# The V half of a gated MLP worked in PSUM from batch 1 on, three remainders moved to GpSimd, and another order of the steps

## The chip, the core and the metric

The kernel runs on one core of a Trainium2 chip. Its time is the device time of one execution in microseconds (us); the time before is the median of 3 runs, 585.59 us (585.12 to 588.33). One more execution was taken by the profiler, and all rows below come from that.

## What is computed

Pooled attention followed by a gated MLP, for 8 batches of 576 positions. Keys and values are averaged over groups of 8 positions; each of 8 heads (64 wide) attends to the 72 pooled keys. The output is the MLP's input `x` (576 x 512).

```python
k_p = k.reshape(B, H, Sp, pool, D).mean(axis=3)
v_p = v.reshape(B, H, Sp, pool, D).mean(axis=3)
attn = softmax(q @ k_p.T / sqrt(D))            # 1e-9 added to the sum
x = (attn @ v_p) as (batch, 576, 512)
h = gelu(x @ w_in)                             # 576 x 1024
u, v = h[..., :512], h[..., 512:]
v_n = (v - mean(v)) / sqrt(var(v) + 1e-6) * g_ln
v_s = w_sg @ v_n + b_sg                        # mixes the 576 positions
out = x + (u * v_s) @ w_out
```

## The kernel before

Every float32 product is made of three products in a rounded form that TensorE takes: a value is written as `hi` (a cast by ScalarE) and a remainder `lo` (value minus `hi`, by GpSimd or VectorE), and hi x hi, hi x lo and lo x hi are added up in PSUM. So nearly every result passes ScalarE and GpSimd once before TensorE can use it.

The work of a batch is cut into named steps, written as generators; each `yield` ends a part. A: load keys, B: load values, C: load queries, E: load the left-over pooled rows, K: pool keys, P: pool values, Q: transpose queries, S: scores and softmax (one for each pair of heads), L and T: transpose the probabilities, V: attention times values, H: the V half of `x @ w_in` with gelu and normalisation, U: the other half with gelu, W: the mixing product with the gate, G and O: the output product (batches 1 to 6 use a form with seven quarter products instead of eight), Z: transpose and store.

Four lists of tokens (PROLOGUE, FIRST, PERIOD, LAST) give the order in which the parts are issued: `H4+0` advances step H4 of the current batch by one part, `S2+1` step S2 of the next. PERIOD is used five times, for batches 2 to 6; the others serve batch 0 (with the conversion of the weights), batch 1 and batch 7. Within each engine the instructions run in the order of the lists, so an instruction that waits holds up all that stands behind it on its engine. All loads and stores are issued on SP's queue, also in this order.

PSUM is handled as four slots `ps` of two banks each. A step takes the slot that has been free the longest (`take`) and returns it (`give`) after the instruction that reads it last.

Step H (from line 712) makes one tile of 128 rows of `x @ w_in` for the V half, in five row tiles H0 to H4. Tile 4 has 64 rows, and its product comes in two halves of the partitions that have to be added. Its parts are: 12 matmuls; for tile 4 a copy of one half to SBUF (L740) and the addition (L742); gelu from PSUM to SBUF (L747, tile 4 L745); statistics `bn_stats` and `bn_aggr` on VectorE (L752, L753) and two small steps on GpSimd for `rstd` (L755, L756); the normalise, one tensor_scalar on VectorE (L758); the cast `hi` on ScalarE (L761); the remainder `lo` (L763), on GpSimd for tiles 0 to 3 and on VectorE for tile 4. From the gelu on the tile lies in SBUF, in a free part of `xmem` (the other batch's input and result) or, for tile 4, in `left`; the slot is given back at the gelu, or for tile 4 at the addition.

Step W (from line 792) mixes the positions: 28 matmuls that read the tiles of H in order, those of tile 4 (`vtail`) last; then the gate on VectorE (L822, L824). Step S: five matmuls for the scores, the maximum (L547), ten exponentials on ScalarE (L566) with their sums, then on VectorE the addition of 1e-9 (L575), the reciprocal (L581) into PSUM beside the scores, the multiply (L584), after which the slot is given back, and two copies `el` on GpSimd (L592). Step P, part 2, makes the pooled values' `vbh` and `vl` (ScalarE, L494 and L508) and their remainders (VectorE, L503 and L510). Step Z transposes on VectorE (L988) into two quarters of `umem` in turn and stores these, so the third and fourth transposes wait for the stores of the first two.

Of the kernel before, what the change touches and what calls it, by code (L numbers as in the profile page):

```python
# [28 lines left out]
T2+0 K2+1 K2+1 B0+1 V3+0 Q1+1 v2 S0+1 V1+0 v2 V3+0 V2+0 C2+1 S0+1 V3+0 P1+1 S0+1 V0+0 S1+1 V2+0 V0+0 C3+1 V3+0 S1+1  # L29
Q2+1 S1+1 lu1 u0 S0+1 S0+1 V2+0 H1+0 u1 S1+1 u0 S0+1 u0 H1+0 u1 S1+1 u0 S1+1 V0+0 H0+0 S0+1 H2+0 S2+1 u1 S1+1 Q3+1  # L30
P0+1 T0+1 V2+0 V1+0 H0+0 u0 u3 u2 u3 u3 H2+0 T0+1 S2+1 S3+1 C0+2 S0+1 H4+0 S3+1 u3 T0+1 S2+1 H3+0 P2+1 S3+1 H4+0 S2+1
H4+0 u3 u2 S3+1 P2+1 u2 H3+0 lo0 S2+1 U1+0 S2+1 S3+1 u2 U3+0 H0+0 H1+0 S2+1 U1+0 S3+1 H4+0 P2+1 U3+0 lo1 u2 H2+0 o0
H3+0 A1+2 o1 H4+0 C2+2 S3+1 H0+0 U0+0 H2+0 H3+0 H0+0 lb0 A0+2 H1+0 o1 H2+0 H4+0 H1+0 P2+1 S3+1 U0+0 U2+0 S2+1 S1+1
H0+0 K0+2 H4+0 o0 E0+2 H4+0 C1+2 H1+0 H2+0 H3+0 L0+1 L0+1 L0+1 U2+0 H3+0 B0+2 L0+1 o1 T1+1 o0 W0+0 K1+2 V0+1 o1 o1
T1+1 V0+1 T1+1 K2+2 o0 o0 o3 o3 W0+0 o3 W3+0 o2 W2+0 V1+1 W3+0 o2 T2+1 T3+1 K2+2 K2+2 o2 V1+1 V0+1 T2+1 W3+0 W0+0 o2
B1+2 Q0+2 W2+0 W2+0 W1+0 T2+1 V2+1 K2+2 K2+2 Q1+2 T3+1 W1+0 W1+0 S1+2 W0+0 W2+0 T3+1 V1+1 S0+2 V2+1 W1+0 P0+2 C3+2
S0+2 o3 V3+1 W3+0 O1+0 C0+3 V3+1 V2+1 V3+1 O1+0 Q2+2 O0+0 O1+0 S1+2 S0+2 o2 Z1+0 O0+0 O0+0 S0+2 S2+2 Z0+0 A0+3 S2+2
# [3 lines left out]
H3+0 O3-1 O3-1 r0 r0 r0 S2+1 r0 H2+0 r0 S1+1 V2+0 P2+1 P2+1 r1 r1 Z1-1 S2+1 K0+2 V0+0 H4+0 r1 P2+1 r1 H1+0 Q0+2 Z2-1
T0+1 H3+0 O3-1 H2+0 H0+0 Z3-1 r3 H4+0 H2+0 Z2-1 H0+0 r3 H3+0 r3 H0+0 S3+1 H4+0 S3+1 H4+0 H1+0 H4+0 S3+1 H3+0 H4+0 H2+0
B0+2 T0+1 r3 H0+0 U1+0 H1+0 U3+0 r2 U2+0 H4+0 H3+0 S3+1 P2+0 U0+0 H0+0 H1+0 H4+0 S0+1 H3+0 H1+0 E0+2 H0+0 H1+0 S3+1
U2+0 U3+0 Z3-1 W1+0 U1+0 r2 K1+2 r2 U0+0 T0+1 r2 r2 K2+2 L0+1 W0+0 W2+0 W1-1 W1+0 W0+0 T0+1 L0+1 L0+1 K2+2 W3+0 W2+0
G0+0 G1+0 L0+1 G0+0 W3+0 L0+1 L0+1 T1+1 V0+1 G1+0 G1+0 S2+0 T2+1 G2+0 G2+0 T1+1 O1+0 T1+1 G2+0 V0+1 G3+0 G4+0 S1+0
V1+1 T2+1 T2+1 K2+2 G2+0 V1+1 G3+0 K2+2 B1+2 O0+0 G2+0 C1+2 T3+1 G4+0 K2+2 C2+2 G3+0 V2+1 O0+0 V2+1 T3+1 G4+0 O0+0
O2+0 O0+0 G4+0 O2+0 V1+1 O0+0 S0+2 T3+1 O0+0 S2+0 O1+0 V3+1 V0+1 O1+0 G4+0 S0+2 O1+0 O0+0 Z0+0 V3+1 Z0+0 Z1+0 O0+0
Z1+0 Z2+0 V3+1 S1-1 Z3+0 Q1+2 V2+1 Z2+0 Z3+0
# [5 lines left out]
S3+1 W1+0 W0+0 P2+1 S2+1 U2+0 S3+1 T0+1 A0+2 W1+0 U3+0 P2+1 T0+1 G1+0 U3+0 W3+0 L0+1 G0+0 G0+0 L0+1 K0+2 K1+2 W2+0
T1+1 P2+1 L0+1 G1+0 L0+1 T2+1 G1+0 W3+0 L0+1 W2+0 G2+0 V0+1 L0+1 G2+0 E0+2 G2+0 T1+1 O1+0 T1+1 V0+1 K2+2 V1+1 T2+1
K2+2 T2+1 O0+0 G3+0 O0+0 G2+0 V1+1 G3+0 W1-5 V2+1 C0+2 T3+1 T3+1 G2+0 T3+1 G3+0 O0+0 G4+0 K2+2 V3+1 O0+0 V2+1 G4+0
O0+0 O0+0 G4+0 O2+0 G4+0 V0+1 O1+0 V3+1 K2+2 O2+0 Q0+2 O1+0 B1+2 K2+2 O1+0 G4+0 Z1+0 O0+0 Z0+0 C2+2 S0+2 O0+0 S0+2
Z0+0 V2+1 V1+1 Z1+0 Z2+0 Z3+0 W0-4 B0+2 Z3+0 Z2+0 V3+1
# [1001 lines left out]
```

## Time and profile before

| | |
|---|---|
| median of 3 runs | 585.59 us |
| the profiled execution | 585.92 us |
| its span (first to last instruction) | 584.1 us |
| mean granted TensorE clock | 0.976 |
| busy: TensorE, VectorE, ScalarE, GpSimd | 95%, 75%, 64%, 58% |

The profile's times are microseconds from the start of the span unless a row says ns. PE is TensorE, DVE VectorE, ACT ScalarE, POOL GpSimd, SP the engine that issues the DMAs. A granted clock of 1.00 is the upper of TensorE's two levels, 2.4 GHz; 0.50 would be the lower, 1.2 GHz. "L758" is line 758 of the kernel; all matmuls have line 133, a helper. `ps` is any of the four slots, `vk` the buffer of the normalised tiles.

### The profile page before, as it was taken

To read this page: it belongs to the slowest core of one execution; us is meant where nothing else is said; L and a number is where in the kernel's file an instruction comes from. 1 tells how busy PE (TensorE), PEld (TensorE's weight loads), DVE (VectorE), ACT (ScalarE), POOL (GpSimd) and SP (SyncE) were. 2 spreads that over 40 slices of the span, in tenths; PEclk is the share of its full clock that TensorE was granted. 3 is DMA by queue.
4 is the path that set the end of the run, shared out by engine and by line. 5 is a ranking of instruction groups with operands and counts; after the bars stand their busy time and mean duration, and the time that the engine had idled before them with its cause. 6 is when DMAs were issued, how large, how long until landed. Compare 5 with 4: busy or idle time off the path is not lost.

```text
span 584.1 us, 10533 instructions
## 1 busy us (share of the span) xinstructions
PE 554.8 (95%) x3675; PEld 518.3 (89%) x3675; DVE 439.5 (75%) x592; ACT 373.1 (64%) x979; POOL 337.9 (58%) x383
## 2 busy tenths in 40 slices
...
GB/s 251 345 183 282 93 75 48 97 115 78 38 82 66 79 96 42 89 128 72 96 26 108 140 41 102 45 99 142 60 82 68 120 81 12 10 1 82 2 1 81
DMA packets 199428, 53.43 MB, mean 91 GB/s; under 512 B 181712, under 2 KB 186896, under 8 KB 199376
## 3 DMA queue, kind: packets, MB, share of 16 engines
...
## 4 chain that ended last, share of the span: by engine, by line
PE 65%; DVE 21%; issue 6%; DMA 2%; ACT 2%; POOL 2%; SPq 1%; DVEq 0%; ACTq 0%; POOLq 0%
PE ps L133 62%; DVE vp L406 4%; DVE left L758 3%; PE ps L169 2%; DVE nmax L547 2%; DVE bst L752 2%; DVE e L584 2%; SPq L221 1%; DMA left<-in_moe_w_sg 1%; DVE xmem L910 1%; DVE xmem L758 1%; DVE vk L763 1%; DMA left<-in_k 1%; DVE qbuf L529 1%; ACT umem L778 1%
## 5 line engine op out<-in xcount | busy, mean ns | idle before, releaser
L133 PE MATMUL ps<-wsh,vk 128*128 128x288 f32 x512 | 105.0, 316 | 4.9 <-DVE e L584 3.4
L133 PEld LDWEIGHTS ps<-wsh,vk 128*128 128x128 f32 x512 | 85.1, 205 | 7.3 <-issue 4.5
L133 PE MATMUL ps<-xhlk,wih 128*128 128x288 f32 x512 | 89.9, 298 | 0.2 <-DVE e L584 0.2
L133 PE MATMUL ps<-wih,xhlk 128*128 128x512 f32 x256 | 84.4, 400 | 0.4 <-DVE al L676 0.2
L566 ACT ACTIVATE e<-ps,nmax 128x72 f32<-128x72 f32 x240 | 73.0, 354 | 12.4 <-DVE nmax L547 12.3
L133 PEld LDWEIGHTS ps<-xhlk,wih 128*128 128x128 f32 x512 | 75.4, 188 | 1.2 <-issue 0.4
L755 POOL TENSOR_TENSOR rstd<-mv,eps 128x1 f32<-128x1 f32 (+1 forms) x40 | 10.2, 256 | 90.8 <-DVE mv L753 73.8
L133 PE MATMUL ps<-wsl,vk 128*128 128x288 f32 x256 | 61.1, 312 | 0.0
L133 PEld LDWEIGHTS ps<-wih,xhlk 128*128 128x128 f32 x256 | 48.1, 188 | 12.5 <-ACT xmem L747 1.0
L566 ACT ACTIVATION_READ_ACCUMULATOR e<-ps,nmax 128x1 f32 x240 | 57.5, 240 | 0.0
L133 PE MATMUL ps<-xhlk,wil 128*128 128x288 f32 x256 | 55.0, 296 | 0.0
L133 PE MATMUL ps<-wil,xhlk 128*128 128x512 f32 x128 | 50.6, 395 | 0.0
L592 POOL COPY el<-e 128x40 f32<-128x40 f32 x64 | 16.6, 322 | 51.7 <-DVE e L584 48.0
L910 DVE TENSOR_TENSOR xmem<-ps,xmem 128x576 f32<-128x576 f32 x42 | 31.4, 748 | 20.0 <-PE ps L133 19.7
L133 PEld LDWEIGHTS ps<-wsl,vk 128*128 128x128 f32 x256 | 46.1, 206 | 0.0
L133 PE MATMUL ps<-gk,woh 128*128 128x288 f32 x224 | 45.9, 296 | 0.0
L708 POOL TENSOR_TENSOR xhlk<-xmem,xhlk 128x576 fp32r<-128x576 f32 x32 | 45.1, 1430 | 1.2 <-ACT xhlk L706 1.2
L133 PE MATMUL ps<-kbd,qbuf 128*128 128x144 f32 x320 | 43.7, 287 | 1.1 <-ACT qbuf L523 0.9
L133 PEld LDWEIGHTS ps<-kbd,qbuf 128*128 128x128 f32 x320 | 41.6, 190 | 2.4 <-ACT qbuf L523 1.0
L854 POOL TENSOR_TENSOR umem<-umem 128x576 f32<-128x576 f32 x24 | 34.9, 1454 | 13.5 <-DVE umem L824 10.2
L763 POOL TENSOR_TENSOR vk<-xmem,vk 128x512 fp32r<-128x512 f32 x32 | 41.6, 1325 | 0.0
L133 PEld LDWEIGHTS ps<-xhlk,wil 128*128 128x128 f32 x256 | 41.0, 188 | 0.0
...
## 6 DMA issues: line engine op xcount, KB each, us to landing
...
```

The lines of the kernel that those rows point to most:

```text
L133: nc.tensor.matmul(o, lhsT, rhs, start=start, stop=stop, **flags)
L169: nc.tensor.transpose(ps[:rows, i * P:(i + 1) * P], src(i), ident if i < NT - 1 else swap)
L406: nc.vector.tensor_reduce(out=o, in_=t.rearrange("p a (r d) -> p a d r", r=POOL), axis=AX.X, op=ALU.add)
L547: nc.vector.tensor_reduce(out=nmax, in_=every.rearrange("p s (h k) -> p s h k", h=2), axis=AX.X, op=ALU.max, negate=True)
L566: nc.scalar.activation(e[:, i, h], slots[i][:, h], AF.Exp, bias=nmax[:, i, h:h + 1], **acc)
L584: (nc.gpsimd if (b, g) in MUL_POOL else nc.vector).tensor_tensor(e, e, rec.unsqueeze(3).broadcast_to([P, NT, 2, SP]), op=ALU.mult)
L592: nc.gpsimd.tensor_copy(st["el", b].rearrange("p t (n j a) -> p t n j a", n=2, a=4)[:, :, g // 2, :, 2 * (g % 2) + h], ef[:, :, LEFT[h]:LE ...
L708: nc.gpsimd.tensor_tensor(xhl[:, 1, g], x32[:, g], xhl[:, 0, g].bitcast(F32), op=ALU.subtract)
L758: nc.vector.tensor_scalar(vg, vg, mv[:, 0:1], rstd, op0=ALU.subtract, op1=ALU.mult)
L763: (nc.gpsimd if i < NT - 1 else nc.vector).tensor_tensor(lo, vg, hi.bitcast(F32), op=ALU.subtract)
L854: nc.gpsimd.tensor_tensor(x, p, q, op=ALU.subtract)
L910: nc.vector.tensor_tensor(x, ps[:, :, 0:HALF], x, op=ALU.add)
```

## The change

From batch 1 on (`old` is batch 0 alone) gelu writes its result back into the slot, statistics and normalise read it there, and the normalise writes to SBUF and gives the slot back. Tile 4's remainder goes to GpSimd from batch 1 on. From batch 2 on (`own`; LEFT_TE holds batches 0 and 1) the remainders `vbl` and `vl` of step P go to GpSimd; as GpSimd's subtraction takes no scale, ScalarE first scales `vp` in place. In the softmax of batches 2 to 7 the addition of 1e-9 writes into PSUM, and the reciprocal works there in place. All four lists hold the same tokens as before in another order; PROLOGUE is the same up to its 141st token.

```diff
@@ step_P
+        own = b not in LEFT_TE
+        if own:
+            nc.scalar.mul(vp, vp, 1.0 / POOL)
         for h in range(2):
             r = slice(D * h, D * h + D)
+            if own:
+                nc.scalar.copy(vbh[r, :, D * h:D * h + D], vp[r])
+                continue
             nc.scalar.mul((vb[b] if b in WHOLE else vbh)[r, :, D * h:D * h + D], vp[r], 1.0 / POOL)
...
+            if own:
+                nc.gpsimd.tensor_tensor(vbl[r, :, D * h:D * h + D], vp[r], vbh[r, :, D * h:D * h + D].bitcast(F32), op=ALU.subtract)
+                continue
...
-        nc.vector.tensor_tensor(vl[64:96], v32, vl[64:96].bitcast(F32), op=ALU.subtract)
+        (nc.vector if b in LEFT_TE else nc.gpsimd).tensor_tensor(vl[64:96], v32, vl[64:96].bitcast(F32), op=ALU.subtract)
@@ step_S
-            nc.vector.tensor_scalar(ssum, ssum, 1e-9, None, op0=ALU.add)
...
-        nc.vector.reciprocal(rec, ssum)
+        if mode:
+            nc.vector.reciprocal(rec, ssum)
+        else:
+            nc.vector.tensor_scalar(rec, ssum, 1e-9, None, op0=ALU.add)
+            nc.vector.reciprocal(rec, rec)
@@ step_H
+        old = b == 0
+        h = vg if old else o[:n]
         if i == NT - 1:
             nc.scalar.copy(vg, o[n:2 * n])
             yield
-            nc.vector.tensor_tensor(vg, o[:n], vg, op=ALU.add)
-            give(bank)
-            yield
-            nc.scalar.activation(vg, vg, AF.Gelu_apprx_tanh)
-        else:
-            nc.scalar.activation(vg, o, AF.Gelu_apprx_tanh)
+            nc.vector.tensor_tensor(h, o[:n], vg, op=ALU.add)
+            if old:
+                give(bank)
+            yield
+        nc.scalar.activation(h, o if old and i < NT - 1 else h, AF.Gelu_apprx_tanh)
+        if old and i < NT - 1:
             give(bank)
...
-        nc.vector.bn_stats(bst, vg)
+        nc.vector.bn_stats(bst, h)
...
-        nc.vector.tensor_scalar(vg, vg, mv[:, 0:1], rstd, op0=ALU.subtract, op1=ALU.mult)
+        nc.vector.tensor_scalar(vg, h, mv[:, 0:1], rstd, op0=ALU.subtract, op1=ALU.mult)
+        if not old:
+            give(bank)
...
-        (nc.gpsimd if i < NT - 1 else nc.vector).tensor_tensor(lo, vg, hi.bitcast(F32), op=ALU.subtract)
+        (nc.gpsimd if i < NT - 1 or b > 0 else nc.vector).tensor_tensor(lo, vg, hi.bitcast(F32), op=ALU.subtract)
```

In the middle batches the matmul parts follow each other so, before and after (one pass of PERIOD: H, U, W and O are of the current batch, T and V, and S1 to S3, of the next, the S0 at the end of the one after):

```
before: H2 H1 H0 S1 H3 H4 U1 U0 S2 S3 U2 W0 W1 U3 W3 W2 T1 T2 V0 O1 V1 O0 V2 T3 O0 V3 O0 O2 O1 O0 S0
after:  H0 H3 H1 H2 S1 U0 H4 U1 S3 S2 U3 U2 W1 W0 W3 W2 T1 T2 V0 O0 V1 O1 V2 T3 O0 V3 O0 O2 O1 S0 O0
```

VectorE's parts in the first half of the pass, from the new list: S0 multiply, H0 statistics, H3 statistics, H0 normalise, H1 statistics, H3 normalise, H1 normalise, S1 maximum, H2 statistics, Q3 and Q2 transposes, H2 normalise, P1 pooling, S1 multiply, H4 addition, S3 maximum, H4 statistics, T0 transpose, H4 normalise, S2 maximum, S3 multiply, P0 pooling, S2 multiply. ScalarE's: S1 exponentials, H4 copy, U0 gelu, H4 gelu, U1 gelu, H2 cast, S3 exponentials, H4 cast, S2 exponentials. GpSimd's before W: H1 and H3 `lo`, H4 `rstd`, H0 and H2 `lo`, S1 and S3 `el`, H4 `lo`, S2 `el`, then step P's three remainders.

## Rows read from the trace of the kernel before

**Rows 1.** The page, busy time, share of the span and instructions of each engine.
```profile
PE 554.8 (95%) x3675; PEld 518.3 (89%) x3675; DVE 439.5 (75%) x592; ACT 373.1 (64%) x979; POOL 337.9 (58%) x383
```
**Rows 2.** Waits of TensorE and VectorE: us in total, times, the longest.
```profile
PE ps L133 <- DVE vk L763: 14.2, 6, 2.5
PE ps L133 <- DVE e L584: 3.6, 6, 0.7
DVE umem L988 <- DMA out<-umem: 24.8, 12, 4.4
```
**Rows 3.** Timelines, batch 6: start, us, engine, instruction [idle before it <- until whom].
```profile
478.43 5.20 DVE L758 TENSOR_SCALAR left<-left,mv,rstd 64x512 f32<-64x512 f32 x1
488.97 0.69 DVE L763 TENSOR_TENSOR vk<-left,vk 64x512 fp32r<-64x512 f32 x1
...
478.37 4.98 POOL L763 TENSOR_TENSOR vk<-xmem,vk 128x512 fp32r<-128x512 f32 x4
...
489.71 0.53 PE L133 MATMUL ps<-wth,vk 128*128 128x288 f32 x2 [2.49 <-DVE vk L763]
```
**Rows 4.** Windows, two W steps each (columns in the rows' order: length, busy, PEclk).
```profile
207.41:220.08 12.67, 9.48 (x58) 9.05 (x57) 12.40 (x17) 12.50 (x50) 2.84 (x6) 0.87 0.33 96
276.30:288.75 12.45, 9.27 (x59) 8.82 (x57) 12.18 (x17) 12.29 (x49) 2.60 (x6) 0.86 0.32 97
344.97:358.76 13.79, 10.68 (x58) 10.16 (x57) 12.97 (x17) 13.00 (x50) 3.13 (x6) 0.75 0.30 89
414.97:427.65 12.68, 9.49 (x58) 9.05 (x57) 12.41 (x17) 12.51 (x50) 2.85 (x6) 0.87 0.29 94
483.85:496.52 12.67, 9.48 (x58) 9.04 (x57) 11.31 (x16) 12.50 (x50) 2.84 (x6) 0.87 0.06 14
291.94:299.41 7.47, 7.47 (x58) 7.47 (x57) 6.08 (x6) 4.19 (x7) 4.23 (x4) 1.00 0.17 51
```
**Rows 5.** Single lines: count, then ns minimum, median and maximum, first and last start.
```profile
L758 DVE TENSOR_SCALAR xmem<-xmem,mv,rstd x32: 495/529/1503, 71.2 to 545.1; 128x512 f32<-128x512 f32 x32
L758 DVE TENSOR_SCALAR left<-left,mv,rstd x8: 531/5201/5205, 74.2 to 547.7; 64x512 f32<-64x512 f32 x8
...
L763 DVE TENSOR_TENSOR vk<-left,vk x8: 684/685/1665, 80.8 to 552.4; 64x512 fp32r<-64x512 f32 x8
...
L910 DVE TENSOR_TENSOR xmem<-ps,xmem x42: 717/757/761, 169.3 to 525.9; 128x576 f32<-128x576 f32 x42
```
**Rows 6.** Lines by form: count | busy us, mean ns of one | idle before.
```profile
L742 DVE TENSOR_TENSOR left<-ps,left 64x512 f32<-64x512 f32 x8 | 5.4, 672 | 0.0
L752 DVE BATCH_NORM_STATS2 bst<-left 64x6 f32<-64x512 f32 x8 | 5.4, 681 | 3.7 <-ACT left L745 3.7
...
L763 POOL TENSOR_TENSOR vk<-xmem,vk 128x512 fp32r<-128x512 f32 x32 | 41.6, 1325 | 0.0
L812 POOL TENSOR_TENSOR gk<-umem,gk 128x288 fp32r<-128x288 f32 x8 | 6.4, 807 | 12.3 <-ACT gk L809 12.3
...
L566 ACT ACTIVATE e<-ps,nmax 128x72 f32<-128x72 f32 x240 | 73.0, 354 | 12.4 <-DVE nmax L547 12.3
L494 ACT ACTIVATE vbh<-vp 64x256 fp32r<-64x256 f32 x14 | 6.1, 436 | 0.4 <-DVE vp L406 0.3
```
**Rows 7.** Windows: three H steps, S1, U3; an H stretch; one whole period.
```profile
457.45:465.94 8.49, 8.49 (x40) 6.86 (x39) 4.22 (x7) 5.20 (x23) 1.14 (x3) 1.00 0.82 146
465.94:467.06 1.12, 1.12 (x11) 1.12 (x10) 0.00 (x0) 0.93 (x3) 0.31 (x1) 1.00 1.04 153
288.75:291.94 3.19, 3.19 (x26) 3.19 (x25) 3.12 (x4) 0.72 (x2) 1.18 (x2) 1.00 0.32 55
...
245.00:264.00 19.00, 18.94 (x103) 16.04 (x102) 12.82 (x24) 13.65 (x52) 7.07 (x9) 1.00 0.74 119
...
245.48:314.15 68.67, 65.43 (x435) 61.48 (x436) 53.82 (x71) 47.73 (x138) 37.86 (x42) 0.98 0.44 87
```
**Rows 8.** VectorE's timeline, the last transpose for a store before batch 6's statistics.
```profile
463.12 0.78 DVE L988 STREAM_TRANSPOSE umem<-xmem 128x576 f32<-128x576 f32 x1 [1.45 <-DMA out<-umem]
```

More of the change, by code (lines that the diff above doesn't have):

```diff
@@ L28 @@
 S3+0 T1+0 s3 C0+1 s3 P0+0 C1+1 L0+0 K0+1 K1+1 T3+0 P2+0 s3 L0+0 v2 V1+0 v3 T3+0 V1+0 B1+1 v2 K2+1 T2+0 Q0+1 u1 u1 V0+0
[L29 to L37, printed above, removed]
@@ L38 @@
-O2+0 S1+2 Q3+2 O2+0 T0+2 V3+1 S2+2 o3 O2+0 V1+1 P1+2 A1+3 H2+1 S0+2 S1+2 P2+2 H2+1 Z0+0
+T2+0 K2+1 K2+1 B0+1 V3+0 Q1+1 v2 V1+0 v2 S0+1 V0+0 V3+0 S0+1 V2+0 C3+1 V2+0 P1+1 u0 S0+1 S1+1 S0+1 P0+1 u0 V0+0 V3+0
+V1+0 V2+0 H2+0 S1+1 u1 P2+1 H0+0 Q3+1 C2+1 u1 H2+0 H0+0 V2+0 u1 lu1 S0+1 S0+1 S1+1 C0+2 u0 S1+1 H2+0 A1+2 H0+0 S0+1
+H3+0 S1+1 Q2+1 u3 H1+0 V0+0 u3 S2+1 S1+1 H3+0 H1+0 T0+1 S1+1 S3+1 V3+0 u0 S2+1 S2+1 S0+1 T0+1 C1+2 u3 T0+1 u3 S3+1 u0
+H0+0 S2+1 u3 H4+0 U1+0 S3+1 H4+0 S2+1 S2+1 H0+0 u2 H4+0 S3+1 U0+0 H2+0 u2 lb0 lo0 H0+0 S2+1 H4+0 U3+0 U1+0 u2 H2+0 u2
@@ new lines @@
+S3+1 S3+1 P2+1 S3+1 S2+1 A0+2 S1+1 P2+1 o1 S3+1 U3+0 u2 H1+0 H3+0 H4+0 K1+2 L0+1 H1+0 U2+0 T2+1 U0+0 P2+1 L0+1 T1+1
+L0+1 U2+0 H3+0 H1+0 V0+1 H3+0 T1+1 L0+1 H2+0 H4+0 H4+0 o1 T1+1 H1+0 E0+2 H4+0 K0+2 H3+0 o0 o0 o1 K2+2 W3+0 V0+1 lo1
+V1+1 V1+1 W1+0 K2+2 B1+2 o0 o1 T2+1 Q0+2 V1+1 o0 W3+0 T2+1 W1+0 W0+0 o1 o0 V2+1 o3 o3 T3+1 o2 o2 W0+0 T3+1 K2+2 B0+2
+o3 o2 K2+2 V2+1 W1+0 T3+1 V0+1 Q1+2 K2+2 W1+0 W2+0 W0+0 V3+1 o2 W3+0 V1+1 W2+0 S0+2 W0+0 S1+2 W2+0 S0+2 C2+2 P1+2 W2+0
+W3+0 O1+0 O1+0 A1+3 S1+2 V3+1 P0+2 o2 C0+3 O1+0 A0+3 O0+0 O0+0 V2+1 O0+0 o3 O2+0 C3+2 S0+2 S1+2 Q2+2 S2+2 S0+2 P2+2
@@ L39 @@
+S2+2 Z0+0 Z0+0 S1+2 V3+1 S2+2 O2+0 H2+1 o3 Z1+0 H2+1 O2+0 S0+2 T0+2 V3+1 Q3+2
 """.split()
 FIRST = """
[L41 to L48, printed above, removed]
+r0 r0 S2+1 O3-1 V0+0 r0 r0 H2+0 H1+0 r0 Z2-1 H2+0 H2+0 K1+2 P2+1 Z1-1 H3+0 O3-1 P2+1 O3-1 S1+1 H0+0 r1 H3+0 S2+0 V2+0
@@ new lines @@
+H4+0 H3+0 H1+0 H0+0 r1 Z3-1 H2+0 H1+0 H3+0 H0+0 H4+0 H4+0 H0+0 r1 S2+0 U2+0 T0+1 r1 S3+1 Z2-1 H3+0 U2+0 H0+0 T0+1 H1+0
+r3 S3+1 H4+0 r3 r3 C1+2 P2+0 H0+0 H3+0 r3 H1+0 H4+0 Z3-1 H1+0 U1+0 U1+0 U3+0 P2+1 r2 S3+1 E0+2 H4+0 K0+2 S3+1 U0+0
+H4+0 S1+0 U0+0 S2+1 B1+2 H4+0 S3+1 W1+0 K2+2 r2 Q0+2 r2 r2 W0+0 T0+1 L0+1 W1+0 r2 S0+1 T0+1 U3+0 W0+0 Q1+2 G1+0 G0+0
+W3+0 L0+1 G0+0 L0+1 W2+0 G1+0 W3+0 L0+1 T1+1 K2+2 W2+0 G2+0 C2+2 T2+1 G1+0 L0+1 L0+1 G2+0 V0+1 T1+1 O0+0 V0+1 G4+0
+G2+0 T1+1 O0+0 K2+2 V1+1 W1-1 T2+1 T2+1 O1+0 G2+0 G3+0 V1+1 T3+1 V2+1 G3+0 G2+0 K2+2 O0+0 G3+0 O0+0 K2+2 V2+1 G4+0
@@ L49 @@
+T3+1 S0+2 V0+1 G4+0 T3+1 O0+0 O0+0 O1+0 B0+2 V2+1 O2+0 S0+2 O2+0 O1+0 O1+0 Z1+0 Z0+0 Z1+0 V3+1 G4+0 G4+0 O0+0 O0+0
+Z0+0 Z3+0 V1+1 Z2+0 Z3+0 Z2+0 V3+1 S1-1 V3+1
 """.split()
 PERIOD = """
-S0+1 H2+0 H1+0 H1+0 H0+0 V0+0 Q2+1 H0+0 V1+0 H2+0 S1+1 V2+0 H1+0 S1+1 V3+0 H1+0 H3+0 H2+0 C3+1 S0+1 H0+0 H4+0 H2+0
-S1+1 H4+0 S1+1 U1+0 H4+0 S1+1 T0+1 H3+0 U0+0 S2+1 H0+0 S0+1 H3+0 T0+1 U1+0 H4+0 H0+0 H2+0 H1+0 H4+0 H3+0 Q3+1 H4+0
-S2+1 S3+1 U0+0 H1+0 P0+1 H3+0 H0+0 H4+0 C1+2 S2+1 S3+1 P1+1 H3+0 S3+1 H2+0 U2+0 P2+1 H4+0 W0+0 S2+1 T0+1 Q1+2 A1+2
@@ L54 @@
[L54 to L58, printed above, removed]
+H0+0 H3+0 S0+1 S0+1 H0+0 H0+0 H3+0 H3+0 H0+0 V0+0 H1+0 H2+0 V2+0 H1+0 H1+0 H0+0 H3+0 S1+1 H1+0 H2+0 V1+0 U0+0 C3+1
```

15 lines of the change are left out of this document (11 added, 4 removed).

## The prediction

> **What bounds the kernel now.** First the page's busy shares: TensorE is busy 554.8 us, 95% of the span [rows 1], so a gain can only come from the 29 us in which it is idle, or from matmuls that ran at the lower clock; the next one, VectorE, is busy for 75%. Second the waits: who keeps TensorE waiting? Half of its idle time stands behind one instruction, the remainder of the fifth row tile, `lo` at L763 (14.2 us in six waits, the longest 2.5), and 3.6 us more behind the softmax multiply L584 [rows 2]. Third the timelines around one such wait, in batch 6 [rows 3]. VectorE's normalise L758 of the fifth tile takes 5.20 us, though the same instruction has a minimum of 0.53 [rows 5]. GpSimd starts four remainders 0.06 us earlier, which run for 4.98 us without a gap; the normalise ends just after they do. So VectorE stands still for 4.7 us. Two score maxima and two pooled reductions are queued behind it on VectorE, ahead of L763, which comes at 488.97; TensorE has by then waited 2.49 us in the middle of step W0 [rows 3], and waits once more for W1's PSUM bank, behind L584 [rows 2].
>
> Fourth, what that costs at the clock: the stretch from the start of W0 to the end of W1, by windows, in the five middle batches [rows 4]. It takes 12.67, 12.45, 13.79, 12.68 and 12.67 us, with a granted clock of 0.75 to 0.87; an undisturbed pair of W steps, the same 56 matmuls, takes 7.47 at 1.00. After the wait the clock falls from the 2.4 to the 1.2 GHz level for a while, and that is in the difference. The five losses are 5.20, 4.98, 6.32, 5.21 and 5.20: **26.9 us** in all.
>
> **The change, part by part.**
>
> *The normalise reads PSUM.* Which VectorE instructions stretch beside GpSimd? Those that read SBUF alone with two tensors, or tensor_scalar: L758 on `xmem` 0.50 to 1.50, on `left` up to 5.21, L763 0.68 to 1.67. The gathers L910, with one operand in PSUM, range from 0.717 to 0.761 over 42 [rows 5], although GpSimd works beside many of them. After the change L758 reads its tile in PSUM, and L763 of the fifth tile runs on GpSimd itself. No row shows a tensor_scalar from PSUM to SBUF. Its ends are 0.53 (the present minimum) and 5.2 (the block stays); I take 0.67, from the 512-column add L742 that reads PSUM [rows 6], as the nearest in operand and size. The block of 4.7 us then goes.
> The Trainium skill, "SBUF — State Buffer", section "Who interferes with whom", says why: VectorE and GpSimd share one port pair under an exclusive lock, and an instruction with at most one SBUF input outside the two-port modes doesn't take it. The 5.20 against 4.98 agree; that a PSUM source frees this instruction no row shows. By the rule the sum below holds; without it, rival C.
> A rule of the Trainium skill speaks against the move: "VectorE: DVE Perf Modes", section "Why PSUM operands drop a tier", says that an fp32 operand in PSUM holds VectorE to its basic rate. By it the normalise goes from 0.53 to 0.67 as taken, 0.14 x 5 = 0.7 us of VectorE a batch, which it has; it would change the sum only if that fell on the path.
>
> *What moves to GpSimd.* From batch 2 on the two `vbl` remainders (64x256), `vl` (32x512) and, from batch 1, the fifth tile's `lo`. By GpSimd's rows (1.33 for 512 columns, 0.81 for 288 [rows 6]) about 2 x 0.75 + 1.3 + 1.3 = 4.1 us a batch. GpSimd's load grows from 37.9 us of a period of 68.7 [rows 7] to some 42 of one of about 64, beside TensorE. VectorE loses these and the block, about 7.5 us a batch. ScalarE gains one scaling of `vp`, 0.44 or a little more by L494 [rows 6]. The L575 add is only rewritten to put its result in PSUM. None of these is on the path by itself.
>
> *Banks are held longer.* There are four two-bank PSUM slots. Before, an H step's slot came back at its gelu; now only after the normalise on VectorE. This is the new wait, and I walked the new list for it. TensorE's prices: H 8.49 / 3 = 2.83, S 1.12, U 3.19, W 7.47 / 2 = 3.74 [rows 4, 7]. With H0's start at 0, the new order puts H2 at 8.5, S1 at 11.3, U0 at 12.4, H4 at 15.6, U1 18.5, S3 21.7, S2 22.8, U3 23.9, U2 27.1, W1 30.3, and W1's last four matmuls, which read the fifth tile, at 33.5. Against this the releases:
> - H2 takes the slot of S0, freed by its multiply L584. VectorE stands first behind the transposes L988, which wait for the previous batch's stores. The last ends at 463.12 + 0.78, 6.45 after the first H step [rows 7, 8]; the softmax tail (0.9 the multiply) takes 1.3: 7.75 against 8.5.
> - S1 takes H0's slot: statistics 0.69 and 0.15, the two small GpSimd steps 0.9, normalise 0.67, with H3's statistics between: 10.2 against 11.3.
> - U0 takes H3's, with H1's statistics ahead of it: 11.7 against 12.4.
> - U2 takes H4's. H4's add comes at 20.5, behind a pooled reduction and S1's multiply; its gelu ends at 21.7 behind U0's and a table load; its statistics stand behind S3's maximum, to 24.8; the T0 transpose is next on VectorE; normalise to 26.4 against 27.1. T0's round trip through DRAM starts after S0's multiply, at about 8, and has 16 us for it; if it took longer, H4's normalise would wait behind it.
> - W1 takes S3's: ten exponentials, up to 3.5 us at 0.354 each, overlapping to about 3.0 [rows 6], behind a table load, then the multiply: 28.7 against 30.3.
> - W1's end needs H4's `lo`: ScalarE's cast stands behind S3's exponentials, to 27.9; on GpSimd S3's `el` copies are queued ahead, to 29.4; 1.3 more: 30.7 against 33.5.
>
> So by this walk every wait is met, with 0.7 to 2.8 us in hand. Loads move on SP's queue too: the `v` load B0, now between two groups of stores, comes ahead of all stores, which costs them nothing once it is issued early; the q load C3 still comes right after them, but VectorE's transpose of it is now due earlier, at about 14, with H2's normalise and so U1's slot (18.5) behind it: 2 us in hand, and I charge nothing.
>
> *The ends.* Batch 0 keeps the old path; its wait (14.2 - 5 x 2.49 = 1.7 us, plus clock) may stay, shrink or grow, since the order around it is new: I take 0, ends -5 and +3. In batch 1 TensorE waited for little; the small GpSimd sums queue ahead of the statistics there, and slots now hang on these: 0 to +3. In batch 7 the normalise's block goes, with some 0.5 us of waits.
>
> **Sum.** 585.9 for the profiled execution (span 584.1 and 1.8 around it), 0.3 above the median of the runs, 585.6, from which I count: 585.6 - 26.9 - 0.5 + 1.8 (one margin of under 1 us overrun by about 0.4 in each of five periods) = **560.0 us**. A period would go from 68.7 to about 64.
>
> **Rivals.**
> - *B: the waits come back at half size.* The order S3 exponentials, H4 cast, S3 `el`, H4 `lo` passes three queues; 3 to 4 us later than read and TensorE waits 1 us at W1, or the banks come 1 us late in the H stretch, with the clock half as long at the lower level as now: about 2 to 2.5 us a period, 570 to 573. For it: margins of 0.7; against: in the kernel before the same queues keep TensorE idle for only 0.06 us in the 19 around the H stretch [rows 7].
> - *C: reading PSUM frees nothing* (the write to SBUF is enough to be blocked), so the normalise still waits out GpSimd. H4's is then 3 us late, U2 and W1 with it: the loss now in W moves ahead: 583 to 588. Against it speak the 42 gathers, which write SBUF too.
> - *D, slower: held banks hand the store wait to TensorE.* VectorE's first H statistics stand behind the transposes that wait for the out DMAs, 4.4 us at the longest [rows 2]. Before, the slots came back without VectorE. If these end later than 7.2 (8.5 less the softmax tail), each us is a us of TensorE in every period, and the lower clock follows. The change turns slower when they are over 3 us later, so that wait and clock cost over 5.4 a period: with 4 us and 3 of clock, 5 x 7 - 27 = 8, 594. Against it: the stores are issued no later than now.
>
> **How the numbers follow.** Forecast 0.66; B 0.16; C 0.07; D 0.08; better than forecast (batch 0's wait goes too, 552 to 555) 0.03. The range takes in the ends of the unknown terms (585.6 - 26.9 - 0.5 - 5 = 553) and B: **553 to 573**, leaving out C and D and a little more. About 0.5% is what a measurement of this kernel can tell from no change: 582.7 to 588.5. Faster 0.85 (forecast, B, better), same 0.07 (C), slower 0.08 (D).
>
> **What would show it.** L758 on the fifth tile near 0.7 us in every batch from 1 on; no wait of TensorE for `vk` in the middle batches; W pairs at 7.5 and the clock at 1.00; period 64. B shows as TensorE waiting for `vk` from GpSimd or for L758; C as L758 of 2 us and more beside GpSimd; D as waits of TensorE for L758 or L584 in the H stretch, with L988 behind out DMAs before. I am wrong if VectorE's share of the path in the H stretch grew by more than the margins above.

## The result, and the profile after

The kernel after takes **558.19 us** (median of 4 runs, 556.94 to 560.35) against 585.36 (584.14 to 588.33) of the kernel before: ratio 0.9533, 95% interval 0.9483 to 0.9582. A second set of runs (experiment 4) gave 557.22 against 587.65, 0.9491 (0.9465 to 0.9517). 560.0 was predicted. The profiled execution took 559.23 us, its span 557.5.

The page of the kernel after: the busy shares, then the chain that ended last, by engine, and below it the same chain of the kernel before. (PEld is TensorE's loading of weights, SPq SP's queue of DMAs; "issue" is time in which an engine waited for nothing that the profile shows.)

```profile
PE 542.0 (97%) x3675; PEld 507.4 (91%) x3675; DVE 399.7 (72%) x567; ACT 377.4 (68%) x987; POOL 352.8 (63%) x408
...
PE 78%; DVE 12%; DMA 3%; issue 2%; SPq 2%; POOL 1%; ACT 1%; DVEq 0%; POOLq 0%
...
PE 65%; DVE 21%; issue 6%; DMA 2%; ACT 2%; POOL 2%; SPq 1%; DVEq 0%; ACTq 0%; POOLq 0%
```

VectorE's share of the chain fell from 21% to 12%. TensorE has the same 3675 matmuls as in [rows 1] and is busy for 12.8 us less, so some of the matmuls have become shorter; 11.1 of the 12.8 lie in the five W pairs below, where the granted clock rose. VectorE lost 39.8 us, GpSimd gained 14.9. Whom does TensorE wait for now? The first rows of its waits in the kernel after (us in total, times, the longest):

```profile
PE ps L302 <- DMA umem<-in_moe_w_sg: 1.7, 1, 1.7
PE ps L133 <- DVE kbd L137: 1.5, 1, 1.5
PE ps L133 <- DVE lt L649: 1.4, 2, 0.9
PE ps L133 <- DVE vk L779: 1.0, 1, 1.0
```

L779 is the old L763. Of the 14.2 us in six waits of [rows 2] one wait of 1.0 is left, in batch 0; the 3.6 us behind the softmax multiply are gone. The four rows shown all lie in the first 180 us. The five W pairs of the middle batches, by windows of the kernel after (columns as in [rows 4]: the window, its length, the busy time and number of instructions of TensorE, its weight loads, VectorE, ScalarE and GpSimd, then the granted clock, the DMA share and GB/s):

```profile
210.86:218.33 7.47, 7.47 (x59) 7.47 (x58) 5.53 (x8) 6.42 (x12) 5.36 (x8) 1.00 0.31 91
274.36:281.83 7.47, 7.47 (x58) 7.47 (x57) 5.70 (x8) 6.58 (x14) 5.36 (x8) 1.00 0.29 90
338.29:345.76 7.47, 7.47 (x58) 7.47 (x57) 5.70 (x8) 6.59 (x14) 5.34 (x8) 1.00 0.31 90
401.96:409.43 7.47, 7.47 (x59) 7.47 (x58) 5.68 (x8) 6.57 (x14) 5.35 (x8) 1.00 0.31 90
465.87:473.34 7.47, 7.47 (x58) 7.47 (x57) 3.19 (x6) 6.58 (x14) 5.34 (x8) 1.00 0.10 22
```

Each is as long as the undisturbed pair of [rows 4], at a granted clock of 1.00 (0.75 to 0.87 before): 64.26 us before, 37.35 now, 26.9 less. To see whether the rest stayed as it was, the two spans are cut at the same matmul of each batch (the first one behind the last gathers of step O). Windows of the kernel before; its second period stands in [rows 7]:

```profile
176.74:245.48 68.74, 65.50 (x436) 61.55 (x434) 53.42 (x70) 47.75 (x135) 38.05 (x42) 0.98 0.39 77
...
314.15:384.16 70.01, 66.85 (x435) 62.83 (x435) 54.18 (x71) 47.68 (x138) 37.83 (x42) 0.95 0.43 86
384.16:453.04 68.88, 65.63 (x436) 61.70 (x436) 53.82 (x71) 47.70 (x138) 37.86 (x42) 0.98 0.43 86
453.04:521.77 68.73, 65.48 (x435) 61.73 (x435) 46.30 (x67) 47.66 (x138) 38.23 (x42) 0.98 0.28 47
```

and of the kernel after:

```profile
176.80:240.30 63.50, 63.38 (x434) 59.97 (x434) 47.32 (x66) 46.90 (x135) 40.53 (x46) 1.00 0.48 94
240.30:304.23 63.93, 63.83 (x435) 60.21 (x435) 47.58 (x67) 48.07 (x138) 40.56 (x46) 1.00 0.48 94
304.23:367.90 63.67, 63.56 (x435) 60.15 (x435) 47.60 (x67) 48.08 (x138) 40.55 (x46) 1.00 0.50 94
367.90:431.81 63.91, 63.79 (x435) 60.19 (x435) 47.49 (x67) 48.07 (x138) 40.56 (x46) 1.00 0.50 94
431.81:495.47 63.66, 63.54 (x436) 60.17 (x436) 40.58 (x62) 49.21 (x140) 40.56 (x46) 1.00 0.23 38
```

The books close: W pairs -26.91, the rest of the five periods +0.55 (345.03 - 318.67 = 26.36), the opening +0.06 (176.80 against 176.74), the end -0.30 (62.03 against 62.33). Together -26.6, which is 557.5 - 584.1. TensorE now idles for 0.1 us of a period by this trace. Of the four terms the opening's is not safe: in a second trace of the same kernel (experiment 4) it ends at 174.53, 2.3 us earlier, while the five periods take 318.64 there, as here.

### The profile page after: what moved, and what is told of

Its sections match the earlier page's. It is cut to its first block, busy times and chain, and to the rows that moved or that the text cites. A ratio compares the mean times of both kernels' runs of the same rounds, so it can differ in the third digit from the quotient of the medians.

```text
span 557.5 us, 10590 instructions
## 1 busy us (share of the span) xinstructions
PE 542.0 (97%) x3675; PEld 507.4 (91%) x3675; DVE 399.7 (72%) x567; ACT 377.4 (68%) x987; POOL 352.8 (63%) x408
## 4 chain that ended last, share of the span: by engine, by line
PE 78%; DVE 12%; DMA 3%; issue 2%; SPq 2%; POOL 1%; ACT 1%; DVEq 0%; POOLq 0%
PE ps L133 76%; DMA left<-in_moe_w_sg 2%; SPq L221 2%; DVE xmem L926 1%; DVE ps L838 1%; DVE al L688 1%; PE ps L169 1%; DMA left<-in_k 1%; DVE tops L269 1%; DVE umem L840 1%; PE ps L302 1%; DVE vp L406 1%; DMA kvraw<-in_k 1%; ACT ah L681 1%; DVE nmax L556 1%
## 5 line engine op out<-in xcount | busy, mean ns | idle before, releaser
L133 PE MATMUL ps<-wsh,vk 128*128 128x288 f32 x512 | 96.6, 296 | 0.5 <-DVE lt L649 0.5
L133 PE MATMUL ps<-wih,xhlk 128*128 128x512 f32 x256 | 82.5, 396 | 0.4 <-ACT xmem L760 0.4
L133 PEld LDWEIGHTS ps<-wsh,vk 128*128 128x128 f32 x512 | 78.3, 188 | 0.7 <-DVE lt L649 0.7
L769 POOL TENSOR_TENSOR rstd<-mv,eps 128x1 f32<-128x1 f32 (+1 forms) x40 | 7.5, 189 | 100.4 <-DVE mv L767 100.4
L133 PE MATMUL ps<-wsl,vk 128*128 128x288 f32 x256 | 57.4, 295 | 0.0
L575 ACT ACTIVATION_READ_ACCUMULATOR e<-ps,nmax 128x1 f32 x240 | 55.2, 230 | 0.0
L779 POOL TENSOR_TENSOR vk<-xmem,vk 128x512 fp32r<-128x512 f32 x32 | 41.5, 1312 | 3.4 <-ACT vk L777 3.3
L133 PEld LDWEIGHTS ps<-wsl,vk 128*128 128x128 f32 x256 | 42.2, 188 | 0.0
L838 DVE SCALAR_TENSOR_TENSOR ps<-ps,gcol,bbc 128x576 f32<-128x576 f32 x28 | 22.7, 809 | 23.3 <-PE ps L133 23.3
```

Source lines behind the costliest of these rows:

```text
L133: nc.tensor.matmul(o, lhsT, rhs, start=start, stop=stop, **flags)
L575: nc.scalar.activation(e[:, i, h], slots[i][:, h], AF.Exp, bias=nmax[:, i, h:h + 1], **acc)
L769: nc.gpsimd.tensor_tensor(rstd, mv[:, 1:2], eps[:n, 1:2], op=ALU.add)
L779: (nc.gpsimd if i < NT - 1 or b > 0 else nc.vector).tensor_tensor(lo, vg, hi.bitcast(F32), op=ALU.subtract)
L838: nc.vector.scalar_tensor_tensor(vs, vs, gcol[:, d:d + 1], bbc.rearrange("p (a n) -> p a n", a=2), op0=ALU.mult, op1=ALU.add)
```

## Experiments

The theory: what cost time was one VectorE instruction, the fifth tile's normalise, standing still beside a run of GpSimd instructions; it is gone because the normalise reads PSUM and because the new order puts fewer GpSimd instructions beside it. The rivals: the new lists and moves carry the gain by themselves; or the queue on VectorE behind the normalise was the cause.

**1. The kernel before, with the fifth tile alone worked in PSUM.**

```diff
-            nc.vector.tensor_tensor(vg, o[:n], vg, op=ALU.add)
-            give(bank)
+            h = vg if b == 0 else o[:n]
+            nc.vector.tensor_tensor(h, o[:n], vg, op=ALU.add)
...
-        nc.vector.tensor_scalar(vg, vg, mv[:, 0:1], rstd, op0=ALU.subtract, op1=ALU.mult)
+        nc.vector.tensor_scalar(vg, h, mv[:, 0:1], rstd, op0=ALU.subtract, op1=ALU.mult)
+        if b > 0 and i == NT - 1:
+            give(bank)
```

> The kernel before with its old lists and one thing changed: from batch 1 on the fifth tile's add, gelu, statistics and normalise work in PSUM, and its slot is given back behind the normalise. My theory (a normalise that reads PSUM is not held up by the four GpSimd remainders that run beside it in this order): L758 on the fifth tile takes 0.8 us beside them, where it took 5.2; the remainder then ends near 485.7 of the old trace, TensorE wants it at 487.1 and slot of W1 at 487.9, so both waits of the five middle W pairs go: 585.4 - 26.9 - 0.5 = 558, range 556 to 563. Rival C (the write to SBUF is held up all the same): L758 stays above 4 us and the time at 583 to 588. Rival L (the new lists and the moves to GpSimd carry the gain): 575 or more.

Measured: 558.72 us (558.22 to 559.4), ratio 0.9538 (0.9496 to 0.958). The old lists are kept, so the run of four GpSimd remainders is still there. Timelines of this kernel, GpSimd and then VectorE, in batch 6:

```profile
456.58 5.00 POOL L768 TENSOR_TENSOR vk<-xmem,vk 128x512 fp32r<-128x512 f32 x4
...
456.65 0.80 DVE L761 TENSOR_SCALAR left<-ps,mv,rstd 64x512 f32<-64x512 f32 x1
```

The same pair as in [rows 3], started 0.07 us apart, and the normalise takes 0.80 where it took 5.20. So it is the source of the operand: the write to SBUF is not held up. Rival C of the prediction falls, and these few lines alone give what the whole change gives: cut as above, the five periods of this kernel take 317.0 us (177.80 to 494.81), those of the kernel after 318.7.

**2. The kernel before with the new lists alone, and the kernel after with its V half back in SBUF.** The first edit replaces PROLOGUE, FIRST, PERIOD and LAST by those of after and nothing else. The second is

```diff
-        old = b == 0
+        old = True
         h = vg if old else o[:n]
```

In both, batch 1's gelu writes into the part of `xmem` that the last transposes of batch 0 still have to read in the new order, so a part of batch 0's output takes other values; the instructions and their sizes stay. (The new lists need the path through PSUM: there `xmem` is written only by the normalise.)

> The kernel before with the new lists alone: normalise from SBUF, remainder of the fifth tile and the V half's on VectorE. In the new order only two GpSimd remainders start beside the fifth tile's normalise, not four. My theory (the block lasts as long as the run of GpSimd instructions): L758 on the fifth tile takes 2.5 us in the middle batches; the slack of 0.8 to 2.9 us covers most of it, but VectorE's own remainder is now the last thing before the tail of W1 (about 469.2 against a want of 469.1 in the trace of after), and the third tile's normalise is stretched too, by up to 1.7, ahead of S1's multiply: 0.5 to 1.5 us of TensorE in a period and as much again by the clock: 561 to 572, taken 565. Rival P (only the read from PSUM brings the gain): 580 or more.

> The kernel after, with the V half's add, gelu, statistics and normalise back in SBUF in all batches; the new lists and the moves to GpSimd stay. My theory: L772 on the fifth tile takes 2.5 us behind two GpSimd remainders, its remainder on GpSimd has 2.9 us in hand and waits for nothing, so only the stretched normalise of the third tile shows, under 1 us a period and its clock: 558 to 567, taken 562. Rival P (the read from PSUM is what brings the gain): 580 or more.

Measured: 562.71 (562.4 to 562.88), ratio 0.9605, for the lists alone; 559.11 (558.04 to 561.73), ratio 0.9547, for lists and moves. Timelines of the first in batch 6, GpSimd and VectorE, and then of the second:

```profile
464.11 2.52 POOL L763 TENSOR_TENSOR vk<-xmem,vk 128x512 fp32r<-128x512 f32 x2
...
464.18 2.74 DVE L758 TENSOR_SCALAR left<-left,mv,rstd 64x512 f32<-64x512 f32 x1
```

```profile
461.79 2.52 POOL L779 TENSOR_TENSOR vk<-xmem,vk 128x512 fp32r<-128x512 f32 x2
...
461.85 2.75 DVE L772 TENSOR_SCALAR left<-left,mv,rstd 64x512 f32<-64x512 f32 x1
```

The normalise from SBUF is still blocked, but for two GpSimd remainders and not for four: 2.74 us. That much the order can bear. Rival P (only the read from PSUM brings the gain) falls too: the lists alone bring most of the gain, and lists and moves nearly all of it. So the gain has two causes of which each is nearly enough, and the kernel after has both. With the lists alone a period takes 64.7 us (from 175.63 to 499.04 in five periods), 1 us more than in the kernel after; with the moves 64.0 (176.33 to 496.49), 0.3 more. Of the 1 us only 0.3 is a wait that the trace names (1.5 us in four waits for the V half's remainder `lt`); the rest is not accounted for.

**3. The kernel after with the moves to GpSimd undone** (both `vbl`, `vl` and the fifth tile's remainder on VectorE again), **and, in a kernel of its own, after with the softmax's small add undone.**

```diff
-                nc.gpsimd.tensor_tensor(vbl[r, :, D * h:D * h + D], vp[r], ...)
+                nc.vector.tensor_tensor(vbl[r, :, D * h:D * h + D], vp[r], ...)
...
-        (nc.vector if b in LEFT_TE else nc.gpsimd).tensor_tensor(vl[64:96], ...)
+        nc.vector.tensor_tensor(vl[64:96], ...)
...
-        (nc.gpsimd if i < NT - 1 or b > 0 else nc.vector).tensor_tensor(lo, ...)
+        (nc.gpsimd if i < NT - 1 else nc.vector).tensor_tensor(lo, ...)
```

```diff
-            nc.vector.tensor_scalar(rec, ssum, 1e-9, None, op0=ALU.add)
-            nc.vector.reciprocal(rec, rec)
+            nc.vector.tensor_scalar(ssum, ssum, 1e-9, None, op0=ALU.add)
+            nc.vector.reciprocal(rec, ssum)
```

> The kernel after with the three moves to GpSimd undone: both vbl remainders, vl and the fifth tile's remainder are on VectorE again, each where the list has it. My theory: the moves were only cover for a full VectorE and none lies on the path by itself; VectorE gets about 4 us a batch back, some of it stretched beside GpSimd; the fifth tile's remainder now ends at about 468.4 against a want of 469.1: 558 to 563, taken 560. Rival M (the moves carry the gain, since VectorE was late by its load): 570 or more.

> The kernel after with one edit undone: the softmax's small add writes its sum to SBUF again and the reciprocal reads it there. All theories: a rewrite of two instructions of 0.17 and 0.23 us that changes nothing of the order: within 1.5 us of the kernel after, 557 to 560.

Measured: 555.97 (555.51 to 557.04) and 557.34 (556.35 to 557.58). The add is worth nothing, as expected, and rival M (570 or more) falls. The moves undone came out 2 us below the kernel after, and below the range that I had given; so they were measured again beside it.

**4. After, after with the moves undone, and after with both undone, in one set of runs.**

> The kernel after once more, unchanged, on the same chip as the next two, so that they are compared within one set of runs: 556 to 560.

> The kernel after with the three moves to GpSimd alone undone, once more beside after. Theory T: within 1 us of after. Rival U: 2 us below it.

> The kernel after with the three moves to GpSimd undone and the softmax's small add back in SBUF. In a single profile each of the undone kernels came out lower than after (undone moves: 553.7 us of span against 557.5), but nearly all of that lay before the sixth of the span's twentieths, in the loading of the first operands. Theory T (the moves and the rewritten add are worth nothing here, the differences are the opening's): within 1 us of after in this set. Rival U (the moves cost time, about 2.2 us): 554 to 556, and 2 us below after in this set.

Measured: 557.22 (556.82 to 558.57) for after, 555.83 (555.1 to 558.42) with the moves undone, 556.67 (556.34 to 556.91) with both undone. The difference is 1.4 and 0.6 us, and the runs of the first two overlap. Theory T holds for the pair undone together and misses by 0.4 us for the moves alone; rival U's 2 us are not there. The traces say where the differences lie: cut as above, the five periods take 318.67 and 318.64 us in two traces of the kernel after, 317.78 and 317.75 in two with the moves undone, and 318.40 with both undone. So in the periods the moves cost at most 0.9 us in all, under 0.2 a period; the rest is the opening, which differs by 2.3 us between the two traces of the kernel after. The moves bring nothing here that can be seen, and no version beat the kernel after by more than these runs can tell.

**5. The kernel before, with the remainder ahead of its queue.** Two tokens of PERIOD moved, H4's remainder forward and P0 behind it; the normalise stays blocked.

```diff
-U0+0 H1+0 P0+1 H3+0 H0+0 H4+0 C1+2 S2+1 S3+1 P1+1 H3+0 S3+1 H2+0 U2+0 P2+1 H4+0 W0+0
+U0+0 H1+0 H3+0 H0+0 H4+0 H4+0 P0+1 C1+2 S2+1 S3+1 P1+1 H3+0 S3+1 H2+0 U2+0 P2+1 W0+0
```

> The kernel before with one token of the middle batches' list moved: VectorE's remainder of the fifth tile (L763) comes ahead of the two pooled reductions and of the second maximum. The normalise stays blocked. My theory (the block holds up both the remainder and the softmax of S2, whose multiply frees W1's slot): the remainder ends near 485.3 and the wait of W0 for it goes, but W1 still gets its slot at about 491.1, where TensorE would want it at 487.9: the wait only changes its name, from L763 to L584, and the time stays at 582 to 587. Rival Q (the queue of two maxima and two reductions ahead of L763 is the cause): 558 to 565.

Measured: 586.47 (median of 10), ratio 1.0045 (0.9998 to 1.0092). A row of TensorE's waits, and timelines of VectorE and TensorE in batch 6:

```profile
PE ps L133 <- DVE e L584: 17.6, 6, 3.5
```

```profile
485.21 0.69 DVE L763 TENSOR_TENSOR vk<-left,vk 64x512 fp32r<-64x512 f32 x1
...
490.91 0.90 DVE L584 TENSOR_TENSOR e<-e,ps 128x720 f32<-128x720 f32 x1
...
487.79 0.43 PE L133 MATMUL ps<-wth,vk 128*128 128x288 f32 x2
...
491.96 0.82 PE L133 MATMUL ps<-wsh,vk 128*128 128x288 f32 x2 [3.48 <-DVE e L584]
```

The remainder is done at 485.90, 1.9 us before TensorE asks for it, and no gain can be seen: W1's slot still comes behind the multiply at 491.8. The 2.49 of W0 and 0.7 of W1 have become 3.48 at W1. The instruction that the waits name was the last to arrive, not the cause.

**6. The kernel before, with the pooled reductions behind the softmax multiplies:** once behind S2's, once behind S3's.

```diff
-P0+1 H3+0 H0+0 H4+0 C1+2 S2+1 S3+1 P1+1 H3+0 S3+1 H2+0 U2+0 P2+1 H4+0 W0+0 S2+1
+H3+0 H0+0 H4+0 C1+2 S2+1 S3+1 H4+0 H3+0 S3+1 H2+0 U2+0 W0+0 S2+1 P0+1 P1+1 P2+1
```

> The kernel before with the middle batches' list changed on VectorE alone: behind the blocked normalise come the two maxima, the fifth tile's remainder and S2's multiply, and only then the two pooled reductions. My theory (the block itself costs TensorE's time, since S2's exponentials cannot start until the cast that waits for the normalise is done): cast until 484.3, table load until 485.6, ten exponentials until 488.7, multiply until about 490.0, where TensorE wants the slot at 487.9: 2.1 us of wait at W1 in place of 2.5 + 0.7, with the clock's part somewhat less: 574 to 581, taken 577. Rival Q (the queue is the cause): 558 to 565.

> The kernel before with the middle batches' list changed on VectorE as in the order that put the two pooled reductions behind S2's multiply, but now behind S3's multiply as well, so that neither softmax waits for them. The normalise stays blocked. My theory (the block alone still costs about 2.5 us of wait at W1, the second wait of that order, 1.8 us behind S3's multiply, was made by the two reductions and goes): 576 to 583. Rival Q (with the queue out of the way the block is harmless): 558 to 565. Rival V (the reductions are as late for the V half as they were for S3, and a third wait comes behind them): 588 or more.

Measured: 593.85 (591.84 to 598.59), ratio 1.0132 (1.005 to 1.0213), and 604.58 (602.85 to 606.73), ratio 1.0294 (1.0257 to 1.033): both slower than before (the first by 0.5 to 2.1%), where I expected 577 and 576 to 583: both forecasts missed. For rival Q they are further off still; rival V's 588 or more is what the second came to. The first, timelines of VectorE and TensorE in batch 6:

```profile
501.64 3.90 DVE L406 TENSOR_REDUCE vp<-kvraw 128x128 f32<-128x1024 f32 x2
...
506.58 0.90 DVE L584 TENSOR_TENSOR e<-e,ps 128x720 f32<-128x720 f32 x1
...
501.87 0.50 PE L133 MATMUL ps<-wsh,vk 128*128 128x288 f32 x2 [2.54 <-DVE e L584]
507.63 1.20 PE L133 MATMUL ps<-xhlk,wih 128*128 128x288 f32 x4 [1.79 <-DVE e L584]
```

The wait at W1 is the forecast one (2.54, with 2.1 walked). The second wait was not walked: both reductions now stand ahead of S3's multiply, which frees U3's slot. The other order removes that one. SP's queue, VectorE and TensorE of it in batch 5:

```profile
438.91 2.52 SPq L221 DMA_DIRECT2D kvraw<-in_k  x4
...
446.71 3.83 DVE L406 TENSOR_REDUCE kp<-kvraw 128x128 f32<-128x1024 f32 x2 [3.88 <-DMA kvraw<-in_k]
...
453.78 0.58 PE L133 MATMUL ps<-ah,vbh 128*128 128x288 f32 x1 [4.32 <-DVE umem L824]
```

and of the kernel before, the same load and reduction in the same batch:

```profile
420.09 2.52 SPq L221 DMA_DIRECT2D kvraw<-in_k  x4
...
429.80 2.02 DVE L406 TENSOR_REDUCE kp<-kvraw 128x128 f32<-128x1024 f32 x1
```

A pooled reduction frees the buffer `kvraw` into which SP loads the next keys. Moved back, it delays that load: issued at 438.91, right behind the reductions, where VectorE asks for it 3.88 us before it is there; in the kernel before it was issued 9.7 us ahead of its reader and nobody waited. Behind the key reductions stand W3's and W2's gates, and TensorE waits 4.32 us for them. Rival V had named a further wait behind late reductions, but not the load that makes it. So these two runs do not price the block by itself, as they were meant to; the wait at W1 is in both (2.53 in the second). They show that the queue could not be moved out of the way.

**7. The kernel after with every normalise issued twice.**

```diff
         nc.vector.tensor_scalar(vg, h, mv[:, 0:1], rstd, op0=ALU.subtract, op1=ALU.mult)
+        if not old:
+            nc.vector.tensor_scalar(vg, h, mv[:, 0:1], rstd, op0=ALU.subtract, op1=ALU.mult)
         if not old:
             give(bank)
```

> The kernel after with the normalise of every V tile from batch 1 on issued twice, 0.8 us more of VectorE for each of five tiles, with the slot given back behind the second. By my walk of the slots (margins of 0.8 to 1.8 us between release and want): U0's slot comes 0.3 late, U1's 1.3 late, S3's about 0.5 late: some 2 us of TensorE in each of six periods, and up to as much again by the clock: 570 to 583, taken 574. Rival R (VectorE is busy for only 72% and has room for 4 us a batch; the margins are wide): 558 to 561.

Measured: 571.11 (570.69 to 573.15), ratio 0.9754 (0.9687 to 0.9821): 4 us a batch on an engine that is busy for 72% cost about 14 us (557.22 in experiment 4). A row of TensorE's waits, and its timeline in batch 6 at U0 and at U1:

```profile
PE ps L133 <- DVE xmem L774: 8.2, 12, 1.2
```

```profile
457.21 0.80 PE L133 MATMUL ps<-xhlk,wih 128*128 128x288 f32 x4 [0.22 <-DVE xmem L774]
...
463.38 0.80 PE L133 MATMUL ps<-xhlk,wih 128*128 128x288 f32 x4 [0.84 <-DVE xmem L774]
```

The two waits stand where the walk puts them (0.3 and 1.3 walked; S3's 0.5 did not come). They are 8.2 of the 14 us; the granted clock is 0.998, so it is not the clock that makes up the rest. In the five middle periods, which grew by 11.5 us against the second trace of the kernel after (330.11 and 318.64), TensorE's busy time grew by 4.6 (322.68 and 318.11) at a granted clock of 1.00 in both: the same matmuls take longer there, and the trace does not show why. Rival R (wide margins) falls: the held slots are the new limit, and the closest of them have about 1 us to spare.

## Why the prediction was right, point by point

**The bound.** TensorE, held by a blocked normalise in each of five W pairs: 26.9 us were to come from there, and 26.91 did. Experiment 1 shows the cause, and experiment 5 that moving the last link of the chain behind the block forward gains nothing. That reading is the one on which all else hung: had I taken the wait's name (`vk` L763) for its cause, the sum would have been the same and the reason wrong.

**The normalise from PSUM.** The two groups of the line in the kernel after that read PSUM (count; ns minimum, median, maximum):

```profile
L772 DVE TENSOR_SCALAR xmem<-ps,mv,rstd x28: 768/809/815, 124.4 to 516.6; 128x512 f32<-128x512 f32 x28
...
L772 DVE TENSOR_SCALAR left<-ps,mv,rstd x7: 802/802/805, 143.6 to 515.8; 64x512 f32<-64x512 f32 x7
```

Mis-sized: 0.80 us and not the 0.67 taken from L742, though no instance is stretched (28 lie within 0.05 us, beside whatever GpSimd does). Against 0.53 from SBUF [rows 5] that is 0.27 x 5 = 1.35 us of VectorE a batch, twice what I gave; it lay beside other work. What the Trainium skill, "SBUF — State Buffer", section "Who interferes with whom", says of an instruction with at most one SBUF input holds here in the form that no row of before had shown: 0.80 us beside four GpSimd remainders (experiment 1). The Trainium skill's sentence on the cost, "VectorE: DVE Perf Modes", section "Why PSUM operands drop a tier", points the right way too: 0.53 became 0.80.

**The moves to GpSimd** were priced at 4.1 us a batch and take that in the second period (two `vbl` 1.5, `vl` 1.3, the remainder 1.3); GpSimd's busy time in it rose by only 2.7 (37.86 [rows 7] to 40.56), since some copies and small steps became shorter (the eight `el` copies 2.0 to 1.6, the five first `rstd` steps 1.4 to 1.0). VectorE's fell by 6.2 in it (53.82 to 47.58), where 7.5 was stated. That they are off the path was right; experiments 3 and 4 put their worth at nothing, or slightly below (0.9 us in five periods at most).

**The walk of the slots.** The timelines of the kernel after in batch 6, VectorE, GpSimd, TensorE; H0 starts at 436.34:

```profile
442.44 0.90 DVE L596 TENSOR_TENSOR e<-e,ps 128x720 f32<-128x720 f32 x1
445.10 0.81 DVE L772 TENSOR_SCALAR xmem<-ps,mv,rstd 128x512 f32<-128x512 f32 x1
446.65 0.78 DVE L772 TENSOR_SCALAR xmem<-ps,mv,rstd 128x512 f32<-128x512 f32 x1
461.08 0.81 DVE L772 TENSOR_SCALAR left<-ps,mv,rstd 64x512 f32<-64x512 f32 x1
463.34 0.90 DVE L596 TENSOR_TENSOR e<-e,ps 128x720 f32<-128x720 f32 x1
...
464.87 1.29 POOL L779 TENSOR_TENSOR vk<-left,vk 64x512 fp32r<-64x512 f32 x1
...
447.54 1.39 PE L133 MATMUL ps<-kbd,qbuf 128*128 128x144 f32 x10
448.67 0.78 PE L133 MATMUL ps<-xhlk,wih 128*128 128x288 f32 x4
462.67 0.70 PE L133 MATMUL ps<-xhlk,wih 128*128 128x288 f32 x4
465.87 0.43 PE L133 MATMUL ps<-wsh,vk 128*128 128x288 f32 x2
469.08 0.43 PE L133 MATMUL ps<-wth,vk 128*128 128x288 f32 x2
```

In us from H0's start, with the release at the end of the row named first:

| step | released by | release: walked, measured | start: walked, measured | margin: walked, measured |
|---|---|---|---|---|
| S1 | H0's normalise | 10.2, 9.57 | 11.3, 11.20 | 1.1, 1.6 |
| U0 | H3's normalise | 11.7, 11.09 | 12.4, 12.33 | 0.7, 1.2 |
| U2 | H4's normalise | 26.4, 25.55 | 27.1, 26.33 | 0.7, 0.8 |
| W1 | S3's multiply | 28.7, 27.90 | 30.3, 29.53 | 1.6, 1.6 |
| tail of W1 | H4's remainder | 30.7, 29.82 | 33.5, 32.74 | 2.8, 2.9 |

H2 likewise: S0's multiply ends at 7.0 (walked 7.75), and TensorE needs it after three H steps. Every wait is met, so no matmul shows one. One price was wrong: H4 has 8 matmuls, not the 12 of the other tiles, and takes 1.9 us (451.96 to 453.83), not the 2.83 of an H step, and all that follows comes 0.8 to 1.0 us early; the releases behind it hang on TensorE's steps and came early with it. Rival D needed the transposes for the stores to end later than 7.2 us; the last ends at 442.06, 5.7.

**The residue.** +1.8 us stood in the sum for margins overrun by 0.4 us; none was, though the rest of the five periods became longer by 0.55 in all. The end: -0.5 taken, -0.30 measured. Batch 0: 0 taken; its wait for `vk` shrank from 1.7 to 1.0 and others came in its place, +0.06 for the opening. So the spans changed by -26.6 us where the sum had -25.6: a miss of 1.0, from 1.25 too much for the residue and 0.26 too little for the two ends. That the median lies 1.8 us below the forecast, just the size of the residue, is chance: the other 0.8 comes mostly from the profiled execution, which lies 1.0 us above the median after and lay 0.3 above the one that the sum counts from. Chance, too, is how near the opening came to the 0 that was taken, since it differs by 2.3 us between two traces of one kernel.

**What I left unsaid:** the forecast treated the read from PSUM as the condition and the lists as the setting. Experiments 1 and 2 show that the read from PSUM alone gives all of it (558.72) and the lists alone most (562.71). So the time by itself could not have told a normalise that is freed from one that is blocked for less: with the V half in SBUF and the rest of the change in place it is 559.11. Rival C was priced too high for the same reason: it had H4's normalise 3 us late, but in the new order two remainders run beside it and not four, and blocked it would have ended 2 us late (an estimate from their end at 463.55 in the trace of after, plus the 0.3 of experiment 2, against 461.89).
